# Inverse Fourier slices, token operands and weight parts of a fused Fourier and two-layer expert kernel, placed elsewhere

## The chip, the cores and the metric

The kernel runs on one core of a Trainium2 chip. The metric is the time on the device in microseconds (us) of one execution, compared by the median of several runs. The core has TensorE (PE in the profile, with its weight loads as PEld), VectorE (DVE), ScalarE (ACT), GpSimd (POOL) and SyncE (SP), which issues all the DMAs of this kernel. Each engine executes its instructions in order.

## The reference

The input `x` is 2 sequences of 3008 rows of 256 numbers. Three things are computed one after the other:

```python
X = np.fft.rfft(x, axis=1)                       # 1. Fourier, complex 256x256 product, shrink, inverse
Yr = Xr @ w_r - Xi @ w_i + b_r ; Yi = Xr @ w_i + Xi @ w_r + b_i
Y = sign(Y) * max(abs(Y) - 0.01, 0)              # real and imaginary part each
x = np.fft.irfft(Y, n=3008, axis=1).reshape(6016, 256)
h = x @ w_in ; x = (h * cos(h)) @ w_out          # 2. first layer, 256 -> 2048 -> 256
h = x @ w_in2 ; out = (h * clip(h + 3, 0, 6) / 6) @ w_out2   # 3. second layer
```

The weights of both layers arrive as 64-bit floats and are converted on the chip.

## The kernel before

**Precision.** A large matrix product is made of three fp32r products: each operand is split in a high part (ACT copies it, which rounds) and a low part (the operand less the high part, one subtraction), and high x high, high x low and low x high are added (`three`, line 754).

**Stage one** (up to about 178 us) holds the forward transform and most of the inverse one. It runs 24 rounds `k2_step(i)`, each with `w_mm` (tile `pp`), `b_mm` (`bp`), `v_mm` (`vp`) and the shrinking between them. What is left of the inverse transform is its last stage: 16 groups `g` of 376 tokens, each in two slices `(g, ec)` of 128 channels. `y_mm` (line 351) makes a slice with four matmuls from `u_sb[g]` and the table `tg_sb[g]` into a PSUM bank, `y_out` (line 363) copies it out on ACT (`yo`), stores it to `x_dram`, and after the second slice of a group issues the loads of `u_sb` and `tg_sb` for the next group (`load_u`). `u_sb` and `tg_sb` have one buffer each. Groups 0 to 4 are done in rounds 16 to 20 of stage one (`Y_EARLY`), the others in stage two.

**Stage two** is the first layer: units `k` = 0 to 47, eight for each of six tiles `jj` of 1024 (the last 896) tokens. A unit has four steps `x` = 0 to 3. In a step `plain(k, x)` makes one block of `h` in PSUM bank `x` with six matmuls; `blk.first()` reads it (ACT L731, DVE L732); the block before it gets its `second()` (ACT Sin L740, DVE product L741, the last reader of its bank); the block two before gets its `split()` (ACT `gh` L747, POOL `gl`); and the block four before is multiplied by the output weights (`out_mm`, tile `acc`, six matmuls). The slices of groups 5 to 15 come one to a unit, in units 1 to 22: `y_mm` in step 2 behind `out_mm`, into bank 0, and `y_out` at the end of step 3. Bank 0 is the bank of the next unit's first block.

**Stage three** (from about 759 us) is the second layer: units 48 to 95, in which seven products replace eight (`seven`): `one()`, `two()` and `last()` fill four banks `h_a` to `h_d`, with sums on DVE between them (L793), and four `out_mm` stand between these.

**Token operands.** `operands(jj)` (line 383) makes the split operands `tok` of the next tile from its staged tokens `st`, in pieces that `prepare(k)` issues in units 3 to 7 of a tile. For a tile of the first layer there are four ACT copies and four subtractions (`halve`); for one of the second layer also sums of tokens: one copy of 512 columns and three of 1024 on ACT, seven `halve` and four subtractions into `st`. All subtractions are `pool_sub` (line 158), so POOL's, and show as L159.

**Weight parts.** `convert` (line 166) turns 512 columns of 64-bit floats into fp32 with DVE bit operations and one POOL sum, and then splits them: `hi()` (ACT L237), `lo()` (POOL), `store()` to DRAM. A part of input weights is split after two such chunks, as 1024 columns in the first layer and 1792 in the second, where four sums of parts come in too (`S1` to `S4`). The `Converter` (line 252) does a chunk in five steps; `cv.step` is called at fixed places in stage one and once in every step of stage two. A chunk's split is done in the third to fifth step of the next chunk. `w_loads(k)` loads the converted weights back, and `require` runs steps until a part is stored. The tile `whi` has one buffer.

**Order.** PE, ACT and SP are in `manual_schedule`: they issue in the order of the program. DVE's and POOL's order is set by the framework's planner from estimated costs.

The lines in question are these:

```python
                if x == 2 and y_late and k > 0:                      # L898
                    y = y_late.pop(0)
                    y_mm(*y, bank(0, f"yp{y[0]}_{y[1]}"))
                elif x == 3 and yp_t:
                    y_out(*y)
```

Of the kernel before, what the change touches and what calls it, by code (L numbers as in the profile page):

```python
# [14 lines left out]
AF = mybir.ActivationFunctionType  # L15
ALU = mybir.AluOpType
# [32 lines left out]
RATE_W = ((2, 1, 2), (0, 0, 1), (0, 1, 1))  # L49
XB, NBIG = 3, 4  # L50
STAGED = [0] * 9 + [1, 2, 4, 5, 7, 8, 10] + [12] * 10
Y_EARLY = range(16, 21)
BIAS_DVE = range(13, 22)


# [67 lines left out]
def fourier_moe_moe_kernel(ctx, tc, x, w_r, w_i, b_r, b_i, ta, tg, fg, win1, wout1, win2, wout2, out):  # L123
# [3 lines left out]
    def f32(ap):  # L127
        return ap.bitcast(F32)
# [29 lines left out]
    def pool_sub(out, x, y):  # L158
        nc.gpsimd.tensor_tensor(out, x, y, op=ALU.subtract)  # L159

    def pool_add(out, x, y):
        nc.gpsimd.tensor_tensor(out, x, y, op=ALU.add)  # L162

    w32 = {}

    def convert(kind, m, c, k):
# [35 lines left out]
        def rest():  # L202
            dve.scalar_tensor_tensor(b, w_lo, float(2.0**-52), b, op0=ALU.mult, op1=ALU.mult)  # L203
            if kind == "o":
                pool_add(a, a, b)
                return
            if k == 0:
                w32[m, c] = persist.tile([128, 8, 256], F32, tag="w32", bufs=1, name=f"w32_{m}{c}")
            w = w32[m, c]
            dst = w[:, A21 : A11 + 1] if k == 0 else w[:, A22 : A12 + 1]  # L210
            pool_add(dst, a.rearrange("p (s f) -> p s f", s=2), b.rearrange("p (s f) -> p s f", s=2))
            if k == 1 and m == 1:
                pool_add(w[:, S1], w[:, A21], w[:, A22])
                pool_sub(w[:, S2], w[:, S1], w[:, A11])
                pool_sub(w[:, S3], w[:, A11], w[:, A21])
                pool_sub(w[:, S4], w[:, A12], w[:, S2])

        def hi():
            if kind == "i":
                s0, ns = SLOTS[m]  # L220
                src = w32[m, c][:, s0 : s0 + ns]
                if direct:
                    t = wi_tile(m, c)
                    dst, low = t[:, 0], t[:, 1]
                else:
                    dst = persist.tile([128, 7, 256], F32R, tag="whi", bufs=1, name=f"whi{name}")[:, :ns]
                    low = src.bitcast(F32R)
            else:
                src = a
                if direct:  # L230
                    t = wo_tile(m, k).rearrange("p z f e -> p z (f e)")
                    dst, low = t[:, 0], t[:, 1]
                else:
                    t = persist.tile([128, 2, 512], F32R, tag="whi", bufs=1, name=f"whi{name}")
                    dst, low = t[:, 0], t[:, 1]
            halves.update(src=src, hi=dst, lo=low)
            act.activation(dst, src, AF.Copy)  # L237

        def lo():
            pool_sub(halves["lo"], halves["src"], f32(halves["hi"]))  # L240

        def store():
            if direct:
# [3 lines left out]
                t = f32(t)  # L247
                sp.dma_start(at[:, z], t.rearrange("p s f -> p (s f)") if kind == "i" else t)

        return dict(load=load, magnitude=magnitude, clamp=clamp, shift=shift, top=top, exponent=exponent, rest=rest, hi=hi, lo=lo, store=store, split=(kind, k) != ("i", 0))  # L250

    class Converter:


        def __init__(self):
            self.queue, self.loaded = [], []
            self.finished = set()
            self.prev, self.last = None, None
            self.course = iter(())

        def add(self, m):
# [9 lines left out]
                ops["load"]()  # L271
                self.loaded.append((key, ops))

        def low(self):
            prev, self.prev = self.prev, None
            if prev:
                prev[1]["lo"]()
                self.last = prev

        def store(self):  # L280
            last, self.last = self.last, None
            if last:
                last[1]["store"]()
                self.finished.add(last[0])

        def chunk(self):
            if self.loaded:
                key, ops = self.loaded.pop(0)
                if not self.prev:
                    ops["magnitude"]()  # L290
                ops["clamp"]()
                yield
                ops["shift"]()
                yield
                ops["top"]()
                if self.prev:
                    self.prev[1]["hi"]()
                yield
                ops["exponent"]()
                self.low()  # L300
                yield
                ops["rest"]()
                self.store()
                if self.loaded:
                    self.loaded[0][1]["magnitude"]()
                yield
                if ops["split"]:
                    self.prev = (key, ops)
                self.load()
            elif self.prev:  # L310
                self.prev[1]["hi"]()
                yield
                self.low()
                yield
                self.store()

        def step(self, n):
            for _ in range(n):
# [64 lines left out]
    def operands(jj):  # L383
# [11 lines left out]
        def at(z, t, count=1):  # L395
            return z[:, t - s0] if count == 1 else z[:, t - s0 : t - s0 + count]

        def halve(t, src):
            pool_sub(at(lo, t), src, f32(at(hi, t)))

        if jj < NJ:
            for e, t in ((0, B11), (1, B21), (0, B12), (1, B22)):
# [8 lines left out]
        halve(B21, st[:, 1, 0])  # L411
        yield
        halve(B22, st[:, 1, 1])
        pool_sub(st[:, 0, 0], st[:, 0, 1], st[:, 0, 0])
        yield
        pool_sub(st[:, 0, 1], st[:, 1, 1], st[:, 0, 1])
        pool_sub(st[:, 1, 1], st[:, 1, 1], st[:, 0, 0])
        act.activation(at(hi, T1, 2), st[:, 0], AF.Copy)
        yield
        pool_sub(st[:, 1, 0], st[:, 1, 0], st[:, 1, 1])  # L420
        halve(T1, st[:, 0, 0])
        halve(T3, st[:, 0, 1])
        act.activation(at(hi, T4, 2), st[:, 1], AF.Copy)  # L423
# [287 lines left out]
    with tc.manual_schedule(engines={mybir.EngineType.PE, mybir.EngineType.SP, mybir.EngineType.Activation}):  # L711
# [39 lines left out]
        def bank(z, name):  # L751
            return psum.tile([128, 512], F32, tag=f"h{z}", bufs=1, name=name)
# [14 lines left out]
        def plain(k, x):  # L767

            f, t = divmod(x, 2)
            h = bank(x, f"h{k}_{x}")  # L770
            blk = Block(k, f, t, h)
            three(h, weights(k, (A11, A21)[f]), tokens(k, (B11, B12)[t]), True, False, blk.n)
            three(h, weights(k, (A12, A22)[f]), tokens(k, (B21, B22)[t]), False, True, blk.n)
            return blk
# [107 lines left out]
        for k in range(G):  # L882
            prepare(k)
            for x in range(4):
                blk = plain(k, x)
                old.append(blk)
                blk.first()
                if len(old) > 2:
                    old[-3].split()
                if len(old) > 1:  # L890
                    old[-2].second()
                for f in pend[:2]:
                    f()
                pend = pend[2:]
                cv.step(1)
                if len(old) > 4:
                    out_mm(old.pop(0))
                if x == 2 and y_late and k > 0:  # L898
                    y = y_late.pop(0)
                    y_mm(*y, bank(0, f"yp{y[0]}_{y[1]}"))  # L900
                elif x == 3 and yp_t:
                    y_out(*y)
            w_loads(k)
        for k in range(G, 2 * G):
            blks, one, two, last = seven(k)
# [71 lines left out]
```

## Time and profile before

| What | Value |
|---|---|
| Median of 3 runs | 1270.52 us (1261.76 to 1274.73) |
| Profiled execution, time on the device | 1268.6 us |
| Its span | 1266.7 us |
| PE busy | 1207.4 us (95%) |
| ACT busy | 774.7 us (61%) |
| POOL busy | 711.7 us (56%) |
| DVE busy | 658.2 us (52%) |
| Chain that ended last | PE 84%, ACT 5%, DMA 4%, POOL 3% |

The span is the time from the first to the last instruction in the trace; the time on the device also holds what lies around it. A busy share is a mean over stages, so the rows below are taken stage by stage. In a timeline row stand the start, the duration, the engine, the line, the operation with the tile written and the tiles read, the shape, the count, and in brackets the idle time before it and what ended that. A row with several instructions of a kind in a row is one merged entry. PE's instructions overlap: a matmul that shows 0.39 us is followed by the next after 0.23.

### The profile page before, as it was taken

The numbers are of one execution on the slowest core, as the hardware profiler recorded it, in microseconds if no ns is written. First come the engines' busy times: TensorE is split into PE (matmuls) and PEld (weight loads), VectorE is DVE, ScalarE is ACT, GpSimd is POOL, SyncE is SP. The second block draws the span as 40 slices with busy tenths as digits, with TensorE's granted clock in tenths as the row PEclk, the third lists the DMA queues.
The fourth block names the chain that finished last, engine by engine and source line by source line (L and its number), as shares of the span: only waits on it lengthen the run. The fifth ranks groups of instructions, "written<-read, shape, count | busy, mean of one in ns | idle before, by whom it ended". The sixth has DMA issues, their size and how long they took to land.

```text
span 1266.7 us, 15833 instructions
## 1 busy us (share of the span) xinstructions
PE 1207.4 (95%) x5520; PEld 1003.9 (79%) x5522; DVE 658.2 (52%) x1007; ACT 774.7 (61%) x1418; POOL 711.7 (56%) x562
## 2 busy tenths in 40 slices
PE   8999899888998989999999899999999999999998
PEld 7888777777776767888888888788787787887897
DVE  3877476755555655555555444444444444444443
ACT  3777476656665666666666565565565665565655
POOL 0434145764666566455454664765756747657644
PEclk9999899999998999999999999999999999999999
DMA  9644666633434412201001442001010010010000
GB/s 243 180 133 125 198 192 226 224 135 110 154 118 134 147 53 101 67 1 37 27 1 65 154 170 107 1 15 52 1 68 0 1 67 1 1 63 1 34 1 29
DMA packets 48007, 108.78 MB, mean 86 GB/s; under 512 B 5972, under 2 KB 22360, under 8 KB 47416
## 3 DMA queue, kind: packets, MB, share of 16 engines
q1 hardware_dynamic: 47928, 107.78, 26.4%
q8 instruction: 43, 0.70, 0.2%
q14 instruction: 36, 0.29, 0.1%
HBM read 65.16 MB, written 42.60 MB: 85 GB/s over the span
## 4 chain that ended last, share of the span: by engine, by line
PE 84%; ACT 5%; DMA 4%; POOL 3%; issue 2%; DVE 1%; SPq 0%; ACTq 0%; POOLq 0%; DVEq 0%
PE acc L756 36%; PE h L756 20%; PE h_b L756 7%; PE pp L541 5%; PE h_a L756 4%; PE h_c L756 2%; PE h_d L756 2%; PE yp L355 2%; PE bp L568 2%; POOL tok L159 2%; PE zp L468 1%; PE vp L607 1%; POOL gl L159 1%; ACT r L740 1%; ACT gh L747 1%
## 5 line engine op out<-in xcount | busy, mean ns | idle before, releaser
L159 POOL TENSOR_TENSOR gl<-r,gh 128x512 fp32r<-128x512 f32 (+1 forms) x384 | 485.2, 1272 | 352.6 <-ACT gh L747 295.1
L756 PE MATMUL acc<-gh,wo 128*128 128x512 f32 (+1 forms) x1536 | 526.9, 389 | 0.0
L756 PEld LDWEIGHTS acc<-gh,wo 128*128 128x128 f32 x1536 | 291.3, 190 | 55.1
L756 PE MATMUL h<-tok,wi 128*128 128x512 f32 (+1 forms) x1152 | 296.7, 393 | 28.5 <-ACT yo L365 28.5
L756 PE MATMUL acc<-gl,wo 128*128 128x512 f32 (+1 forms) x768 | 300.3, 391 | 14.5 <-POOL gl L159 14.5
L756 PEld LDWEIGHTS h<-tok,wi 128*128 128x128 f32 x1152 | 215.6, 190 | 76.8 <-ACT yo L365 37.8
L731 ACT ACTIVATE r<-h 128x512 int32<-128x512 f32 (+1 forms) x192 | 113.0, 589 | 205.5 <-PE h L756 197.0
L732 DVE SCALAR_TENSOR_TENSOR r<-r,h 128x512 f32<-128x512 int32 (+1 forms) x192 | 129.7, 675 | 201.5 <-ACT r L731 201.4
L747 ACT ACTIVATE gh<-r 128x512 fp32r<-128x512 f32 (+1 forms) x384 | 231.2, 615 | 2.7 <-DVE r L741 2.6
L756 PEld LDWEIGHTS acc<-gl,wo 128*128 128x128 f32 x768 | 145.8, 190 | 48.7 <-POOL gl L159 21.5
L741 DVE TENSOR_TENSOR r<-r,h 128x512 f32<-128x512 f32 (+1 forms) x192 | 129.7, 676 | 58.9 <-ACT r L740 58.8
L756 PE MATMUL h_b<-tok,wi 128*128 128x512 f32 (+1 forms) x432 | 120.1, 386 | 0.5 <-DVE h_d L793 0.5
L740 ACT ACTIVATE r<-r 128x512 f32<-128x512 f32 (+1 forms) x192 | 117.8, 613 | 0.0
L159 POOL TENSOR_TENSOR tok<-st,tok 128x512 fp32r<-128x512 f32 (+1 forms) x66 | 83.3, 1274 | 46.6 <-ACT tok L423 14.2
L793 DVE TENSOR_TENSOR h_b<-p,h_b 128x512 f32<-128x512 f32 (+1 forms) x48 | 32.9, 685 | 129.6 <-PE h_b L756 116.8
L756 PEld LDWEIGHTS h_b<-tok,wi 128*128 128x128 f32 x432 | 80.6, 188 | 16.9 <-DVE h_d L793 2.2
L756 PE MATMUL h_a<-tok,wi 128*128 128x512 f32 (+1 forms) x288 | 80.0, 386 | 0.0
L789 ACT ACTIVATE p<-h_a 128x512 f32<-128x512 f32 (+1 forms) x48 | 28.3, 590 | 74.3 <-PE h_a L756 74.3
L756 PEld LDWEIGHTS h_a<-tok,wi 128*128 128x128 f32 x288 | 54.4, 189 | 10.3
L735 DVE SCALAR_TENSOR_TENSOR r<-r,h_a 128x512 f32<-128x512 f32 (+1 forms) x48 | 32.4, 676 | 54.1 <-ACT r L734 54.1
L735 DVE SCALAR_TENSOR_TENSOR r<-r,h_b 128x512 f32<-128x512 f32 (+1 forms) x48 | 32.5, 677 | 54.0 <-ACT r L734 54.0
L162 POOL TENSOR_TENSOR w<-cvai,cvbi 128x512 f32<-128x512 f32 x16 | 21.2, 1324 | 68.0 <-DVE cvbi L203 65.7
(100 smaller groups left out, 1385.1 us busy)
## 6 DMA issues: line engine op xcount, KB each, us to landing
st<-x_dram SPq DMA_DIRECT2D x20, 512.0 KB, 5.5
rawi<-in_win_dram SPq DMA_DIRECT2D x16, 512.0 KB, 4.3
rawo<-in_wout_dram SPq DMA_DIRECT2D x16, 512.0 KB, 4.5
wo_dram<-whio SPq DMA_DIRECT2D x28, 256.0 KB, 2.0
wo<-wo_dram SPq DMA_DIRECT2D x14, 512.0 KB, 6.2
wi<-wi_dram SPq DMA_DIRECT2D x4, 1792.0 KB, 7.0
u_dram<-v SPq DMA_DIRECT2D x48, 128.0 KB, 2.4
u_sb<-u_dram SPq DMA_DIRECT2D x16, 384.0 KB, 4.4
```

What stands on the lines that cost most here:

```text
L159: nc.gpsimd.tensor_tensor(out, x, y, op=ALU.subtract)
L355: pe.matmul(yp[:, i * TP : (i + 1) * TP], lhsT=u_sb[g][:, i, ec * 128 : (ec + 1) * 128], rhs=tg_sb[g][:, i * TP : (i + 1) * TP], start=Tru ...
L541: pe.matmul(pp.rearrange("p a e -> p (a e)"), lhsT=za[:, p, kc, 2 * (k2 % 2) : 2 * (k2 % 2) + 2, :].rearrange("p r n -> p (r n)"), rhs=wb[ ...
L731: act.activation(q, h, AF.Copy, bias=0.25, scale=1.0 / TWO_PI)
L732: dve.scalar_tensor_tensor(r, q, -TWO_PI, h, op0=ALU.mult, op1=ALU.add)
L735: dve.scalar_tensor_tensor(r, r, 6.0, h, op0=ALU.min, op1=ALU.mult)
L740: act.activation(r, r, AF.Sin, bias=math.pi / 2, scale=1.0)
L741: dve.tensor_tensor(r, r, self.h[:, : self.n], op=ALU.mult)
L747: act.activation(gh[:, :n], self.r[:, :n], AF.Copy)
L756: pe.matmul(h[:, :n], lhsT=w, rhs=x, start=start and j == 0, stop=stop and j == 2, skip_group_check=True)
L789: act.activation(r[:, :n], h[:, :n], AF.Copy)
L793: dve.tensor_tensor(h[:, :n], r[:, :n], x[:, :n], op=ALU.add)
```

## The change

1. `Y_EARLY` becomes rounds 16 to 18: groups 0 to 2 stay in stage one, groups 3 to 15 go to stage two.
2. In stage two a unit takes two slices, in steps 1 and 2, from unit 0 on: `y_mm` follows `plain` at once, into bank 3 in step 1 and bank 0 in step 2, and `y_out` follows in the same step, behind `second`. The 26 slices fill units 0 to 12.
3. The subtractions in `operands` go from POOL to DVE.
4. A chunk's split begins in the first step of the next chunk. Input weights are split in pieces of two slots (512 columns), one piece a step, each piece's POOL subtraction issued one step behind its ACT copy. The four sums of a second-layer part take one step each. `store` comes behind the last subtraction. `magnitude` is issued once for every chunk; before, the second chunk of a part had it twice.

```diff
-Y_EARLY = range(16, 21)
+Y_EARLY = range(16, 19)
...
-            if k == 1 and m == 1:
-                pool_add(w[:, S1], w[:, A21], w[:, A22])
-                pool_sub(w[:, S2], w[:, S1], w[:, A11])
-                pool_sub(w[:, S3], w[:, A11], w[:, A21])
-                pool_sub(w[:, S4], w[:, A12], w[:, S2])
+        def sums():
+            if kind == "i" and k == 1 and m == 1:
+                w = w32[m, c]
+                for op, z, x, y in ((pool_add, S1, A21, A22), (pool_sub, S2, S1, A11), (pool_sub, S3, A11, A21), (pool_sub, S4, A12, S2)):
+                    op(w[:, z], w[:, x], w[:, y])
+                    yield
...
-            act.activation(dst, src, AF.Copy)
-        def lo():
-            pool_sub(halves["lo"], halves["src"], f32(halves["hi"]))
+        def pieces():
+            place()
+            src, hi, lo = (halves[z] for z in ("src", "hi", "lo"))
+            last = None
+            for z in range(0, src.shape[1], 2) if kind == "i" else (None,):
+                cut = (lambda t: t[:, z : min(z + 2, src.shape[1])]) if kind == "i" else (lambda t: t)
+                if last:
+                    pool_sub(*last)
+                act.activation(cut(hi), cut(src), AF.Copy)
+                last = cut(lo), cut(src), f32(cut(hi))
+                yield
+            pool_sub(*last)
+            yield
+            store()
...
         def chunk(self):
+            tail = self.tail()
             if self.loaded:
                 key, ops = self.loaded.pop(0)
-                if not self.prev:
+                if not self.begun:
                     ops["magnitude"]()
...
+                for part in ("clamp", "shift", "top", "exponent", "rest"):
+                    ops[part]()
+                    next(tail, None)
+                    if part == "rest":
+                        for _ in tail:
+                            pass
+                        if self.loaded:
+                            self.loaded[0][1]["magnitude"]()
+                    yield
+                self.begun = bool(self.loaded)
+                yield from ops["sums"]()
...
+        def sub(out, x, y):
+            dve.tensor_tensor(out, x, y, op=ALU.subtract)
         def halve(t, src):
-            pool_sub(at(lo, t), src, f32(at(hi, t)))
+            sub(at(lo, t), src, f32(at(hi, t)))
...
                 blk = plain(k, x)
+                y = y_late.pop(0) if y_late and x in (1, 2) else None
+                if y:
+                    y_mm(*y, bank(3 if x == 1 else 0, f"yp{y[0]}_{y[1]}"))
                 old.append(blk)
                 blk.first()
                 if len(old) > 2:
                     old[-3].split()
                 if len(old) > 1:
                     old[-2].second()
+                if y:
+                    y_out(*y)
...
-                if x == 2 and y_late and k > 0:
-                    y = y_late.pop(0)
-                    y_mm(*y, bank(0, f"yp{y[0]}_{y[1]}"))
-                elif x == 3 and yp_t:
-                    y_out(*y)
```

`tail()` runs the `pieces()` of the chunk before and marks it as finished when `store` has been issued. The four other `pool_sub` in `operands` (those into `st`) become `sub` in the same way.

## Rows read from the trace of the kernel before

**Rows 1.** Busy time by stretch: start and end, length, each engine's busy time, granted clock.

```profile
200.00:300.00 100.00, 89.09 (x396) 71.32 (x395) 63.42 (x92) 61.52 (x112) 65.86 (x50) 0.97 0.53 179
500.00:600.00 100.00, 100.00 (x443) 82.81 (x442) 50.54 (x74) 66.43 (x124) 53.74 (x42) 1.00 0.10 35
```

**Rows 2.** What PE waited for in the whole span: total us, times, longest.

```profile
PE h L756 <- ACT yo L365: 28.5, 22, 3.3
PE acc L756 <- POOL gl L159: 14.5, 10, 2.4
PE yp L355 <- DMA tg_sb<-in_tg_dram: 4.5, 3, 2.0
```

**Rows 3.** Timeline of PE, starts of units 2 and 23 and the steps around.

```profile
196.58 1.66 PE L756 MATMUL h<-tok,wi 128*128 128x512 f32 x6 [0.78 <-ACT yo L365]
...
483.86 1.03 PE L355 MATMUL yp<-tg_sb,u_sb 96*128 96x94 f32 x8
...
486.14 0.40 PE L756 MATMUL acc<-gh,wo 128*128 128x512 f32 x1
...
488.46 1.66 PE L756 MATMUL h<-tok,wi 128*128 128x512 f32 x6 [0.78 <-ACT yo L365]
...
491.32 1.52 PE L756 MATMUL h<-tok,wi 128*128 128x512 f32 x6
...
494.04 1.52 PE L756 MATMUL h<-tok,wi 128*128 128x512 f32 x6
```

**Rows 4.** Timeline of all engines in stage two, around steps and slices.

```profile
199.44 1.52 PE L756 MATMUL h<-tok,wi 128*128 128x512 f32 x6
...
202.73 0.69 DVE L741 TENSOR_TENSOR r<-r,h 128x512 f32<-128x512 f32 x1 [0.35 <-ACT r L740]
...
208.95 0.47 ACT L365 ACTIVATE yo<-yp 128x376 f32<-128x376 f32 x1
...
210.78 0.41 SPq L346 DMA_DIRECT2D tg_sb<-in_tg_dram  x1
...
259.20 1.13 PE L355 MATMUL yp<-tg_sb,u_sb 96*128 96x94 f32 x8 [0.57 <-DVE r L741]
```

**Rows 5.** The tile `tg_sb`: its sixteen loads, from issue to landing.

```profile
DMA to landing us min/median/max: 3.8/4.3/4.8
```

**Rows 6.** Timeline of PE in the last rounds of stage one.

```profile
140.41 0.47 PE L541 MATMUL pp<-wh,zh 128*128 128x512 f32 x1
...
147.25 3.41 PE L355 MATMUL yp<-tg_sb,u_sb 96*128 96x94 f32 x16 [1.79 <-DMA tg_sb<-in_tg_dram]
...
158.88 0.48 PE L541 MATMUL pp<-wh,zh 128*128 128x512 f32 x1
...
163.75 0.39 PE L541 MATMUL pp<-wh,zh 128*128 128x512 f32 x1
...
176.20 1.43 PE L568 MATMUL bp<-ph,fgr 128*128 128x512 f32 x5 [0.95 <-DVE ph L555]
```

**Rows 7.** The chain that ended last, stage three: start, duration, work; one row a unit.

```profile
786.05 2.72 PE acc L756 x12
796.25 2.72 PE acc L756 x12
...
1160.82 2.72 PE acc L756 x12
```

**Rows 8.** Timeline at the end of stage two and in stage three, POOL and PE.

```profile
721.96 0.48 PE L756 MATMUL acc<-gl,wo 128*128 128x448 f32 x1 [2.40 <-POOL gl L159]
...
804.93 2.53 POOL L159 TENSOR_TENSOR tok<-st,tok 128x512 fp32r<-128x512 f32 x2
...
808.73 0.50 PE L756 MATMUL acc<-gl,wo 128*128 128x512 f32 x1 [2.05 <-POOL gl L159]
```

**Rows 9.** Line 601, `sl` on DVE: count, shortest, median and longest in ns.

```profile
L601 DVE TENSOR_TENSOR sl<-u,sh x24: 677/692/1940, 41.1 to 180.9; 128x512 fp32r<-128x512 f32 x24
```

**Rows 10.** Groups by shape: the subtraction of second-layer input weights on POOL.

```profile
L159 POOL TENSOR_TENSOR w<-w,whii 128x1792 fp32r<-128x1792 f32 x4 | 16.2, 4038 | 3.6 <-ACT whii L237 3.6
```

More of the change, by code (lines that the diff above doesn't have):

```diff
@@ L211, in rest, with place @@
             pool_add(dst, a.rearrange("p (s f) -> p s f", s=2), b.rearrange("p (s f) -> p s f", s=2))
-            if k == 1 and m == 1:
-                pool_add(w[:, S1], w[:, A21], w[:, A22])
-                pool_sub(w[:, S2], w[:, S1], w[:, A11])
-                pool_sub(w[:, S3], w[:, A11], w[:, A21])
-                pool_sub(w[:, S4], w[:, A12], w[:, S2])
-        def hi():
+        def sums():
[4 more added lines that the diff above has]
+                    yield
+        def place():
             if kind == "i":
@@ L248, in store @@
                 sp.dma_start(at[:, z], t.rearrange("p s f -> p (s f)") if kind == "i" else t)
-        return dict(load=load, magnitude=magnitude, clamp=clamp, shift=shift, top=top, exponent=exponent, rest=rest, hi=hi, lo=lo, store=store, split=(kind, k) != ("i", 0))
+        return dict(load=load, magnitude=magnitude, clamp=clamp, shift=shift, top=top, exponent=exponent, rest=rest, pieces=pieces, sums=sums, split=(kind, k) != ("i", 0))
     class Converter:
@@ L257, in __init__ @@
             self.finished = set()
-            self.prev, self.last = None, None
+            self.prev, self.begun = None, False
             self.course = iter(())
@@ L272, in load, with tail @@
                 self.loaded.append((key, ops))
-        def low(self):
+        def tail(self):
             prev, self.prev = self.prev, None
             if prev:
[L277 to L284, printed above, removed]
+                yield from prev[1]["pieces"]()
+                self.finished.add(prev[0])
         def chunk(self):
+            tail = self.tail()
             if self.loaded:
                 key, ops = self.loaded.pop(0)
-                if not self.prev:
+                if not self.begun:
                     ops["magnitude"]()
[L291 to L306, printed above, removed]
+                for part in ("clamp", "shift", "top", "exponent", "rest"):
[9 more added lines that the diff above has]
+                yield from ops["sums"]()
                 if ops["split"]:
@@ L309, in chunk @@
                 self.load()
[L310 to L315, printed above, removed]
+            else:
+                yield from tail
         def step(self, n):
@@ L413, in operands @@
         halve(B22, st[:, 1, 1])
[L414 removed]
+        sub(st[:, 0, 0], st[:, 0, 1], st[:, 0, 0])
         yield
[L416 to L417 removed]
+        sub(st[:, 0, 1], st[:, 1, 1], st[:, 0, 1])
+        sub(st[:, 1, 1], st[:, 1, 1], st[:, 0, 0])
         act.activation(at(hi, T1, 2), st[:, 0], AF.Copy)
         yield
[L420 removed]
+        sub(st[:, 1, 0], st[:, 1, 0], st[:, 1, 1])
         halve(T1, st[:, 0, 0])
```

## The prediction

> **What bounds the kernel now.** I read the busy shares by stretch first, then what TensorE (PE) waited for, then the timeline of single units. From 500 to 600 us PE is busy all the time; between 200 and 300 us it is busy for 89.09 us of 100, while VectorE, ScalarE and GpSimd (DVE, ACT, POOL) are at 62 to 66 [rows 1]. So PE is the bound throughout, and only its idle time and what follows from it can be won. The list of PE's waits names three that this change touches: 28.5 us in 22 waits for the copy `yo` on ACT, 14.5 us in 10 waits for `gl` on POOL, 4.5 us in 3 waits for the table `tg_sb` [rows 2].
>
> The named wait is not its whole price. In stage two a step without a y slice takes 494.04 - 491.32 = 2.72 us, so a unit of four steps 10.88. A y slice adds 486.14 - 483.86 = 2.28 less the 1.36 us (half a step) of the six `h` matmuls behind it, so 0.92: a unit with one slice should take 11.80. Unit 2 begins at 196.58 and unit 23 at 488.46: 21 units in 291.88 us, 13.90 each [rows 3]. The excess is 2.10 us a unit, of which the named wait is 28.5 / 22 = 1.30. The other 0.80 is the pipeline running empty and filling again, a few waits for DVE and POOL, and slower matmuls after long waits (granted clock 0.97 in the mean [rows 1]).
>
> **The change part by part.** Sums are made against the profiled execution: 1268.6 us, 1.9 above its span of 1266.7 and 1.9 below the median of the three runs.
>
> *y slices.* Before, the copy was the last ACT work of step 3 while the next unit's first block needs the same PSUM bank 0 at once. Now slices sit in steps 1 and 2, their copies are issued in the same step, and the banks (3, then 0) are needed again only two steps later, over 5 us. The 22 waits go, with the excess around them: 22 x 2.10 = **-46.2**. What is late next? First, bank 3 at step 1: its last reader is the DVE product (L741) of the block before, issued one step earlier. In a quiet stretch, counted from a step's first matmul at 199.44, that product ends at 203.42 and `plain` of the next step ends issuing at 199.44 + 2.72 + 1.36 = 203.52: a margin of 0.1 us, and one such wait of 0.57 is already there at 259.20 [rows 4]. Weight conversion or a token operand ahead of L741 on DVE turns it into a wait. Bounds: nothing, or 1.30 for each of 26 slices (the old wait's size), 34. I take 0.4 at the 13 step-1 slices, **+5**, near the one row that shows it; at step 2 the slice just before gives DVE 0.92 more. Second, the loads of the next group: each group now has one unit, and `u_sb` and `tg_sb` have one buffer. The copy will start when the Sin pass ends, about 202.7 on the same scale; from the copy's start to the issue of `tg_sb` SP took 210.78 - 208.95 = 1.83 us behind two stores [rows 4], and landing takes 4.3 us, at most 4.8 [rows 5]. So the table is there at 208.8 to 209.3; PE wants it one slice and six half steps after 200.8, at 209.9. Margin 1.1 to 0.6. Ahead of this load on SP stand the converter's raw loads and stores and, after units 0, 2 and 4, the weight loads, each waiting for its own producer. Bounds 0 and 12 x 2.0 (the longest such wait in rows 2); I take 12 x 0.25 = **+3**.
>
> *Four slices moved from stage one.* They cost 4 x 0.92 = **+3.7** later. In stage one the two rounds that lose them took 158.88 - 140.41 = 18.47 us, one with a wait of 1.79 for the table and then slow matmuls (3.41 for 16); the round after them, without a slice, took 163.75 - 158.88 = 4.87 [rows 6]. That gives back 18.47 - 9.74 = **-8.7**. The two earlier waits for the table stay.
>
> *Token operands.* 90 subtractions (66 into `tok`, 24 into `st`) leave POOL for DVE. In stage three, POOL does the two `tok` ones at 804.93 for 2.53 us, ahead of a `gl` that PE needs, and PE waits 2.05 us at 808.73; there are five such places [rows 8]. From 796.25 to 1160.82 stand 34 units of 796.25 - 786.05 = 10.20 us, 346.8, in 364.57 us: 17.8 lost [rows 7]. With POOL holding nothing but `gl`, `gl` follows its copy. DVE gets 11 subtractions a tile; the nearest row with the same operands, `sl`, has a median of 0.692 and a maximum of 1.940 us [rows 9]. DVE is the engine whose `h_c` sum the last product of a unit waits on, so a group of them placed ahead of that sum is the next delay. DVE's order is the planner's, not the program's, as POOL's was, so the group may be pulled together. Bounds -17.8 and 0; I take 1 us a tile as given back: **-12.8**. The same at the end of stage two: the wait of 2.40 at 721.96 [rows 8] goes, **-2.4**. At the end of stage one four halves join a DVE for which PE already waits 0.95 at 176.20 [rows 6], but the same four leave a POOL that they held: bounds -1 and +5, I take **+2**.
>
> The `sl` row shows the dispute: its median is 0.692, and the 1.940 runs beside a POOL subtraction [rows 9]. The Trainium skill ("SBUF — State Buffer", section "Who interferes with whom") says that a VectorE instruction with two SBUF inputs and a GpSimd instruction that reads SBUF exclude each other, whichever began first holding the pair of ports; by that each moved subtraction can also hold up a `gl`, which no token work on DVE did before, and the token term would shrink towards 0. Median against maximum speaks for a collision in a minority of cases.
>
> *Weight parts.* A POOL piece of 1792 columns, 4.038 us, four times [rows 10], becomes pieces of 512 and one of 256, and the four sums of a second-layer part come one a step; a `gl` no longer queues behind 4 us. PE's `gl` waits in stage two are few, so this gains little. Copies (Abs) issued twice fall away, off the path. Against it: the first piece's ACT copy now comes one step behind the POOL sum that it reads, where it came three steps behind; in rounds 2 to 7 of stage one both are issued in one call, so ACT, in order, waits there with the next `ph` copy behind it. And a second-layer part's `whi` buffer is claimed again one step after its store is issued. PE's four rotating banks cover a microsecond or two of that. Four more converter steps per second-layer part make conversion end about five units later, still eleven before its weights are wanted; the converter's forced steps at unit 4 fall from five to three. Bounds -3 and +6; I take **+2**.
>
> Sum: -46.2 + 5 + 3 + 3.7 - 8.7 - 12.8 - 2.4 + 2 + 2 = -54.4: 1214.2 on 1268.6, so **1216** against the median.
>
> **The rivals.**
> 1. *The bank wait takes the copy's place.* DVE's L741 is late at both slices of a unit. For it: the margin of 0.1 and the 0.57 at 259.20. Against: the wait is bounded by DVE's one product, and step 2 has a margin of about 1 us. At 1.30 x 26 = 34 instead of 5: 1245. Chance 0.12.
> 2. *DVE becomes the late engine.* The token group, at up to 1.940 each, delays the `h_c` sums and the new `gl`; stage three and the end of stage two gain nothing: 1216 + 15.2 = 1231. For it: POOL's order had just such groups. Against: DVE's share there is under half and a subtraction costs half of POOL's. Chance 0.20.
> 3. *Only the named waits go.* The 0.80 a unit beyond the wait belongs to other engines and stays: 22 x 0.80 = 17.6 back, 1234. Chance 0.15.
> 4. *Slower: late group loads.* Twelve loads in line on SP, behind stores that wait for POOL. It passes the old time when each load is late by 54.4 / 12 = 4.5 us beyond my 0.25, and slower by 1% at 5.6; at 6 us it is 1216 + 72 = 1288. For it: one unit per group instead of two. Against: landings of 4.3 us with little spread and a margin of 1. Chance 0.05; a partial form (2 us each, 1240) lies in the range.
>
> My forecast's case has 0.48. The range is **1200 to 1243**: low, no new waits (-8) and -5 more of the third stage's loss; high, rivals 2 and 3 and the milder half of rival 1. Changes under 1% can't be told from none here. Faster by over 1%: 0.89; within 1%: 0.06, where two rivals add up; slower: 0.05.
>
> **What would show it.** After the change, PE's waits hold no `h` behind `yo`; units with two slices take about 12.7 + 0.6 us and there are 13 of them; the units after them take 10.88. A wait of `yp` for `r` L741 in over half of the slices at over 1 us is rival 1; `yp` waiting for `tg_sb` or `u_sb` in most units is rival 4. In stage three no `acc` behind `gl` and tiles about 82 us apart; `h_b` or `acc` waiting behind DVE is rival 2. If stage one does not shorten by about 7 us, the moved subtractions or the earlier copies cost there. The forecast is wrong if the 13.90 us units stay above 12.9 without slices in them.

## The result, and the profile after

The kernel after takes **1215.47 us** (median of 4 runs, 1211.86 to 1221.14), where the runs of the kernel before beside it have a median of 1266.14: ratio 0.96, interval 0.9524 to 0.9677. The profiled execution took 1211.86 us with a span of 1210.1, so its span is 56.6 us shorter; the sum had said 54.4. By the medians 50.7 us are gained, and 55.1 when the kernel after was run a second time (experiment 10).

The page after: the lines to set against the small table of before. DVE has gained 84 us of work and POOL has lost 98, ACT is much as it was, and POOL is gone from the chain. PE does the same 5520 matmuls in 17.8 us less (1207.4 before), with a mean granted clock of 0.997 in place of 0.987; so of the 56.6 us some 39 are idle time of PE and the rest are faster matmuls.

```profile
PE 1189.6 (98%) x5520; PEld 995.8 (82%) x5522; DVE 742.1 (61%) x1097; ACT 770.5 (64%) x1426; POOL 613.4 (51%) x488
PE 85%; DVE 6%; DMA 5%; ACT 2%; issue 1%; SPq 0%; ACTq 0%; DVEq 0%
```

What PE waited for in the whole span after (total us, times, longest). Against [rows 2]: the 28.5 us for `yo` are gone, the 14.5 for `gl` too. The first row is the bank wait that the prediction named (PE waits for the last reader of the bank that a slice needs).

```profile
PE yp L354 <- DVE r L743: 6.0, 5, 2.4
...
PE h_b L758 <- DVE h_d L795: 2.1, 5, 0.5
PE yp L354 <- DMA tg_sb<-in_tg_dram: 1.5, 2, 1.0
PE h_d L805 <- DVE r L743: 1.4, 1, 1.4
```

Busy time by stretch after (columns as in [rows 1]): the stretch that had 10.91 us of idle PE has 5.70. In the third row, six microseconds that begin just before the longest bank wait ends, the granted clock is 0.72.

```profile
200.00:300.00 100.00, 94.30 (x452) 77.88 (x451) 60.35 (x86) 63.07 (x121) 57.98 (x47) 0.97 0.61 201
500.00:600.00 100.00, 100.00 (x443) 82.80 (x442) 54.17 (x79) 65.07 (x121) 49.04 (x39) 1.00 0.08 26
234.00:240.00 6.00, 5.43 (x22) 4.48 (x22) 5.92 (x8) 2.21 (x4) 3.79 (x3) 0.72 0.66 179
```

PE's timeline after. The first and last rows are marks used below: the first output product (in unit 1) and the last stage's first wait in unit 48. Between them stand the slice behind the one with the longest wait (239.91, used further down), a unit with two slices, 329.90 - 317.11 = 12.79 us from slice to slice, and a step without one, 341.35 - 338.63 = 2.72.

```profile
176.31 0.39 PE L758 MATMUL acc<-gh,wo 128*128 128x512 f32 x1
...
239.91 1.02 PE L354 MATMUL yp<-tg_sb,u_sb 96*128 96x94 f32 x8
...
317.11 1.08 PE L354 MATMUL yp<-tg_sb,u_sb 96*128 96x94 f32 x8
...
329.90 1.08 PE L354 MATMUL yp<-tg_sb,u_sb 96*128 96x94 f32 x8
...
338.63 1.52 PE L758 MATMUL h<-tok,wi 128*128 128x512 f32 x6
...
341.35 1.52 PE L758 MATMUL h<-tok,wi 128*128 128x512 f32 x6
...
714.10 0.50 PE L805 MATMUL h_d<-tok,wi 128*128 128x512 f32 x1 [1.42 <-DVE r L743]
```

The chain that ended last, stage three after: the 34 units of [rows 7] now take 1103.79 - 750.99 = 352.8 us, where they took 364.57 and 346.8 would be the floor.

```profile
750.99 2.72 PE acc L758 x12
...
1103.79 2.72 PE acc L758 x12
```

With these marks every run can be cut into three stretches: **stage one** up to the first output product (unit 0, with its two slices after the change, lies in it, which the description of the kernel before counts to stage two), **stage two** from there to the wait in unit 48, **stage three** from there to the end. This table has the profiled execution of each kernel; "idle" is the length of stage two less PE's busy time in it. The kernel after, run a second time, gave 537.84 for stage two against 537.79. That they agree so well is partly luck, since the idle time in it differs by 1.3 and the matmuls by as much the other way; stage one repeats less well (experiment 7 says why). Every row is one execution, on several chips, and the profiled one of the kernel before took 1268.6, where its runs beside the four changes tried on their own have a median of 1264.46. So these four rows gain 4 to 8 us more over the first row, all stages together, than their medians do.

| Kernel | Stage one | Stage two | idle in it | Stage three |
|---|---|---|---|---|
| before | 185.2 | 573.75 | 35.0 | 507.8 |
| slices alone | 181.1 | 555.01 | 18.1 | 505.3 |
| copy alone | 186.2 | 548.79 | 15.8 | 506.2 |
| tokens alone | 182.6 | 564.49 | 30.7 | 496.5 |
| weight parts alone | 183.2 | 571.08 | 35.2 | 507.3 |
| slices + tokens | 178.7 | 557.30 | 21.0 | 495.5 |
| slices + weight parts | 179.6 | 543.50 | 10.8 | 507.0 |
| **after** (all three) | 176.3 | 537.79 | 7.3 | 496.0 |
| after, again | 177.4 | 537.84 | 8.6 | 497.3 |
| after, weights uncut | 187.1 | 540.74 | 10.6 | 497.2 |
| after, `st` on POOL | 179.4 | 538.92 | 8.7 | 500.7 |
| after, slices later | 180.8 | 532.13 | 5.0 | 495.8 |
| after, steps spread | 178.9 | 534.81 | 6.0 | 495.7 |
| **after, later + spread** | 179.1 | 529.21 | 2.7 | 495.9 |

### The profile page after: what moved, and what is told of

It is laid out like the page before. It is cut to its first block, busy times and chain, and to the rows that moved or that the text cites. A ratio compares the mean times of both kernels' runs of the same rounds, so it can differ in the third digit from the quotient of the medians.

```text
span 1210.1 us, 15853 instructions
## 1 busy us (share of the span) xinstructions
PE 1189.6 (98%) x5520; PEld 995.8 (82%) x5522; DVE 742.1 (61%) x1097; ACT 770.5 (64%) x1426; POOL 613.4 (51%) x488
## 4 chain that ended last, share of the span: by engine, by line
PE 85%; DVE 6%; DMA 5%; ACT 2%; issue 1%; SPq 0%; ACTq 0%; DVEq 0%
PE acc L758 38%; PE h L758 20%; PE h_b L758 7%; PE h_a L758 4%; PE pp L543 4%; PE h_d L758 2%; PE h_c L758 2%; PE yp L354 2%; PE bp L570 2%; DVE tok L398 1%; DVE st L398 1%; PE vp L609 1%; DVE r L737 1%; PE zp L470 1%; DMA x_big<-in_ta_dram 1%
## 5 line engine op out<-in xcount | busy, mean ns | idle before, releaser
L159 POOL TENSOR_TENSOR gl<-r,gh 128x512 fp32r<-128x512 f32 (+1 forms) x384 | 492.7, 1291 | 439.3 <-ACT gh L749 387.1
L758 PE MATMUL acc<-gl,wo 128*128 128x512 f32 (+1 forms) x768 | 296.7, 386 | 0.0
L758 PE MATMUL h<-tok,wi 128*128 128x512 f32 (+1 forms) x1152 | 290.0, 387 | 0.0
L398 DVE TENSOR_TENSOR tok<-st,tok 128x512 fp32r<-128x512 f32 (+1 forms) x66 | 62.1, 954 | 4.6 <-ACT tok L406 1.7
```

Source lines behind the costliest of these rows:

```text
L398: dve.tensor_tensor(out, x, y, op=ALU.subtract)
L758: pe.matmul(h[:, :n], lhsT=w, rhs=x, start=start and j == 0, stop=stop and j == 2, skip_group_check=True)
```

## The experiments

Ratios are against runs of the kernel before made beside them on the same chip, with 95% intervals; diffs are against the kernel named. Lists of PE's waits in stage two count from 165 us on (178 with the copy alone), so that they hold unit 0.

**1. Slices alone** (against before: `Y_EARLY` and the loop of stage two).

```
-Y_EARLY = range(16, 21)
+Y_EARLY = range(16, 19)
+                y = y_late.pop(0) if y_late and x in (1, 2) else None
+                if y:
+                    y_mm(*y, bank(3 if x == 1 else 0, ...))
...
+                if y:
+                    y_out(*y)
-                if x == 2 and y_late and k > 0: ...
-                elif x == 3 and yp_t: ...
```

> Of the whole change only the slices: groups 0 to 2 early, two slices a unit in steps 1 and 2. Theory A (the whole excess of 2.10 us a unit comes from the copy that holds bank 0): 42 to 46 us faster, ratio 0.964 to 0.967, no wait of h for yo, units after unit 12 at 10.88 us. Theory B (only the named 1.30 us a unit goes, the other engines own the rest): 24 to 28 us faster, ratio near 0.98. Both: the waits of PE for gl of 10 us in the second layer stay.

Measured: 1244.97 us, 0.9854 (0.983 to 0.9878). Neither number was met; at 1.5% the gain is under half of what the slices' terms had said (-43 us with stage one, 3.4%). PE's waits in stage two, slices alone:

```profile
PE yp L355 <- DVE r L741: 9.1, 6, 4.7
PE acc L756 <- POOL gl L159: 5.6, 4, 2.5
PE yp L355 <- DMA tg_sb<-in_tg_dram: 2.2, 1, 2.2
```

The `yo` wait is gone as foreseen; 16.9 us of other waits stand in its place, where before had 5.1 (4.5 for `gl`, 0.6 for L741) besides the `yo` ones. Around the longest, all engines, slices alone:

```profile
238.47 0.63 ACT L237 ACTIVATE whio<-cvao 128x512 fp32r<-128x512 f32 x1 [2.51 <-DMA wo_dram<-whio]
...
240.35 0.67 ACT L188 ACTIVATE cvai<-rawi 128x512 f32<-128x512 f32 x1 [1.24 <-POOL w L162]
...
242.05 0.69 DVE L732 SCALAR_TENSOR_TENSOR r<-r,h 128x512 f32<-128x512 int32 x1 [3.07 <-ACT r L731]
...
243.82 2.02 PE L355 MATMUL yp<-tg_sb,u_sb 96*128 96x94 f32 x8 [4.71 <-DVE r L741]
```

ACT, in order, stands 2.51 us for a `whio` buffer whose store has not ended and 1.24 for a POOL sum; both are converter work, issued in a burst because unit 4's part is due. The block's own ACT work stands behind them, DVE waits for it, and PE for DVE. The slice then runs at half speed (2.02 against 1.03, granted clock 0.50). That the `yo` waits of the kernel before covered such bursts is inferred, not shown.

**2. The copy alone** (against before: still one slice a unit, in step 2, but made right behind the block's matmuls, ahead of the output product, and copied in the same step).

```
+                y = y_late.pop(0) if y_late and x == 2 and k > 0 else None
+                if y:
+                    y_mm(*y, bank(0, ...))
...
+                if y:
+                    y_out(*y)
-                if x == 2 and y_late and k > 0: ...
-                elif x == 3 and yp_t: ...
```

> One edit to the kernel before: one slice a unit as before (units 1 to 22, step 2, bank 0), but it is made right behind the block's matmuls and copied in the same step; groups 0 to 4 stay early. Theory A (the place of the copy is the cause, not how many slices a unit has): 36 to 44 us faster, ratio 0.966 to 0.972, units 1 to 22 at 11.8 us. Rival (the wait moves to the bank's last reader on DVE): 22 waits of yp for L741 at about 1.3 us, under 10 us faster, ratio above 0.992.

Measured: 1243.2 us, 0.9846 (0.9819 to 0.9873), between the two expectations and as good as two slices a unit. So the gain comes from where the slice is made and copied, not from putting two into a unit. Made and copied earlier are one edit here; in experiment 9 ("later") the matmuls are behind the output product again, only the copy stays earlier, and no `yo` wait returns. Timeline of PE with the copy alone:

```profile
191.89 1.13 PE L355 MATMUL yp<-tg_sb,u_sb 96*128 96x94 f32 x8
...
203.80 1.08 PE L355 MATMUL yp<-tg_sb,u_sb 96*128 96x94 f32 x8
...
244.82 2.02 PE L355 MATMUL yp<-tg_sb,u_sb 96*128 96x94 f32 x8 [5.25 <-DVE r L741]
```

A quiet unit takes 203.80 - 191.89 = 11.91, near the 11.80 of the prediction, so there the whole excess did go. But stage two is only 25.0 us shorter, not 46.2, and its waits say why (copy alone):

```profile
PE yp L355 <- DVE r L741: 9.2, 4, 5.3
PE acc L756 <- POOL gl L159: 4.9, 4, 2.4
```

**3. Tokens alone** (against before; likewise in the four lines that write `st`).

```
+        def sub(out, x, y):
+            dve.tensor_tensor(out, x, y, op=ALU.subtract)
         def halve(t, src):
-            pool_sub(at(lo, t), src, f32(at(hi, t)))
+            sub(at(lo, t), src, f32(at(hi, t)))
```

> Only the token subtractions go from POOL to DVE. Theory A: about 14 us faster (11.8 in the second layer as in the changed kernel, 2.4 at the end of the first), ratio 0.989, and the waits of h for yo stay at about 28 us in 22 places. Rival (two subtractions on DVE and POOL exclude each other and DVE becomes late): within 3 us of before, ratio 0.998 to 1.002, gl late as before.

Measured: 1249.04 us, 0.9885 (0.9858 to 0.9911), as expected. PE's waits with tokens alone, whole span: the `gl` waits of 14.5 us are down to 0.3, `yo` stays, and the price on DVE is the last row. Three token subtractions on DVE take 3.78 to 3.83 us, each beside a POOL weight subtraction of 4.01 to 4.06; no bank wait of PE comes of it here, other than in experiment 5.

```profile
PE h L759 <- ACT yo L365: 28.9, 22, 3.3
...
PE h_b L759 <- DVE h_d L796: 2.4, 6, 0.5
```

**4. Weight parts alone** (against before: `place`, `pieces`, `sums` and the converter's `chunk` and `tail` as in the change's diff, nothing else of it).

```
-                if self.prev:
-                    self.prev[1]["hi"]()
...
+                for part in ("clamp", "shift", "top", "exponent", "rest"):
+                    ops[part]()
+                    next(tail, None)
...
+                yield from ops["sums"]()
```

> Only the weight parts in pieces, one step earlier. Theory A (nearly nothing, the few long yo waits behind the 1.7 us ACT copy get shorter): 0 to 6 us faster, ratio 0.995 to 1.0. Rival (the ACT copy right behind the POOL sum stalls stage one): slower by 3 to 8 us, ratio 1.002 to 1.006. Third theory (the stall of POOL by 4 us parts was a large part of the excess in stage two): over 10 us faster, ratio below 0.992.

Measured: 1263.28 us, 0.9994 (0.9975 to 1.0012): nothing, as expected. Its `yo` waits are the old ones, 30.4 us in 22:

```profile
PE h L755 <- ACT yo L364: 30.4, 22, 5.1
PE acc L755 <- POOL gl L159: 13.4, 9, 2.4
```

The three singles together give 1.46 + 1.15 + 0.06 = 2.67%, the whole 4.0%. So some parts do something together that none does alone; the pairs say which.

**5. Slices + tokens** (against after: the weight parts' functions back as before).

```
-                    next(tail, None)
-                yield from ops["sums"]()
...
+                if self.prev:
+                    self.prev[1]["hi"]()
...
+                self.low()
```

> Slices and token operands changed, weight parts as before. The slices alone were 1.5% faster, the tokens 1.2%, the weight parts 0.1%, the whole 4.0%: some 1.3% exist only together. Theory A (the earlier, smaller weight pieces shorten the waits of the slices for L741): this kernel gets 30 to 36 us of the whole 51, ratio 0.972 to 0.976, with a wait of yp near 4.7 us at unit 5 as in the slices alone. Theory B (it is POOL's relief that the slices need): 45 us or more, ratio below 0.966, no wait over 2.5 us there.

Measured: 1232.97 us, 0.9718 (0.9697 to 0.974), as theory A said. By time the two about add up (2.6% from the singles, 2.8% here), but not by stage: in stage two this kernel is 2.3 us longer than slices alone, though tokens alone had taken 9.3 off there. PE's waits in stage two, slices + tokens, and the timeline of one:

```profile
PE yp L355 <- DVE r L744: 16.6, 5, 4.9
PE acc L759 <- POOL gl L159: 2.4, 3, 1.5
```

```profile
266.30 4.01 POOL L159 TENSOR_TENSOR w<-w,whii 128x1792 fp32r<-128x1792 f32 x1 [0.77 <-ACT whii L237]
...
266.77 4.09 DVE L399 TENSOR_TENSOR tok<-st,tok 128x512 fp32r<-128x512 f32 x1 [1.42 <-ACT tok L407]
...
272.11 1.41 PE L355 MATMUL yp<-tg_sb,u_sb 96*128 96x94 f32 x8 [3.77 <-DVE r L744]
```

POOL's uncut weight subtraction runs from 266.30 to 270.31, and the token subtraction on DVE, 0.69 at its median, ends at 270.86, after 4.09 us. The next L744 is late and PE stands 3.77. The same three rows return at 340.47, 340.88 and 346.28 (4.01, 4.15 and 3.84 us). These two waits are most of what the tokens add, where slices alone has 0.70 at each; of the others, 4.92 at unit 5 and 2.78 at unit 9 were there with slices alone (4.71 and 2.54). This is the exclusion that the prediction cited from the Trainium skill ("SBUF — State Buffer", section "Who interferes with whom"); the trace agrees, and shows it at its most expensive: the DVE instruction ends 0.55 us after the POOL one, whenever it began.

**6. Slices + weight parts** (against after: the token operands back on POOL, those of `st` too).

```
-            sub(at(lo, t), src, f32(at(hi, t)))
+            pool_sub(at(lo, t), src, f32(at(hi, t)))
```

> Slices and weight parts changed, token subtractions on POOL as before. Theory A: the whole less what the tokens give alone, 34 to 38 us faster, ratio 0.970 to 0.973, with gl late in the second layer as before and no gl wait in the slices' units. Theory B: about 20 us faster, ratio 0.983 to 0.986.

Measured: 1232.03 us, 0.9714 (0.9691 to 0.9738), as theory A said, where 1 and 4 would add to 1.5%: weight parts alone show 2.7 us of stage two, which their time can't tell from nothing, behind moved slices 11.5 (555.01 to 543.50), and with the tokens moved too 19.5 (557.30 to 537.79). Of the 11.5, 7.3 are idle time of PE and 4.2 faster matmuls. PE's waits in stage two, slices + weight parts:

```profile
PE yp L354 <- DVE r L740: 5.0, 4, 2.8
PE acc L755 <- POOL gl L159: 3.4, 2, 2.4
PE yp L354 <- DMA tg_sb<-in_tg_dram: 1.1, 1, 1.1
```

**7. After, weights uncut** (against after: the steps in their new places, each POOL and ACT instruction in one piece).

```
-            for z in range(0, src.shape[1], 2) if kind == "i" else (None,):
-                cut = (lambda t: t[:, z : min(z + 2, src.shape[1])]) if ...
+            for z in (None,):
+                cut = lambda t: t
```

> The changed kernel with the input weights of a part split in one ACT copy and one POOL subtraction of 1024 or 1792 columns, all else of the new order kept. Theory (a subtraction with two SBUF operands on DVE waits out the POOL instruction beside it, 4.0 us at 1792 columns, so the pieces are what the token operands on DVE need): 7 to 14 us slower than the changed kernel, token subtractions of about 4 us on DVE, waits of yp for L743 over 3 us in two of units 6 to 12. Rival (the gain of the weight part is its earlier place, not the cut): within 2 us of the changed kernel.

Measured: 1224.34 us, 0.9645 (0.9605 to 0.9686), against 1214.11 for the kernel after beside it. Ten microseconds, within the 7 to 14 that were expected, but not for the reason given, and not all of them are the cut's. The profile's first stretch, weights uncut:

```profile
0.00:30.00 30.00, 26.73 (x126) 23.58 (x128) 7.24 (x14) 7.71 (x15) 0.20 (x4) 0.68 0.92 239
```

Its granted clock there is 0.68, where the kernel after had 1.00 and, run again, 0.94, with the same instructions so far. PE's 161st matmul starts at 38.7 us here and at 28.7 in the second run, and its 891st 9.6 us later: the 9.7 us by which stage one is longer than the second run's 177.4 were lost before the first of these. Stage two, where the cut acts, is 2.9 us longer, with four `gl` waits of 2.4 us in all that after does not have; stage three is equal. Two token subtractions took 4.13 and 4.14 us, but stood after the slices, so the long `yp` waits that were expected did not come. The profile shows about 3 us for the cut; the two of its six runs with the highest mean clock (0.996 and 0.995) took 1219.74 and 1220.22, 3 to 7 above the kernel after's 1213.09 to 1216.35. Its full price stays open. What is left of the weight parts' 19.5 us is put down to the steps' new places: sums one a step, pieces from the first step of the next part on, three forced steps at unit 4 instead of five. No run took these apart, so this is argued, but number 9 bears on the forced ones.

**8. After, `st` on POOL** (against after; the four subtractions into `st` alone).

```
-        sub(st[:, 0, 0], st[:, 0, 1], st[:, 0, 0])
+        pool_sub(st[:, 0, 0], st[:, 0, 1], st[:, 0, 0])
...
-        sub(st[:, 1, 0], st[:, 1, 0], st[:, 1, 1])
+        pool_sub(st[:, 1, 0], st[:, 1, 0], st[:, 1, 1])
```

> The changed kernel with the four subtractions into st of each second-layer tile back on POOL, the seven into tok kept on DVE. Theory (in the second layer DVE's group of subtractions now is the late one, 0.48 us at h_b a tile): h_b waits go and up to 3 us are gained. Rival (POOL's order again puts them ahead of gl): waits of acc for gl of about 1 to 2 us in five places, 3 to 9 us slower than the changed kernel.

Measured: 1220.46 us, 0.962 (0.9587 to 0.9652), 6.3 above the kernel after. The size is the rival's, but the wait is another: hardly `gl` (1.5 us in 2), but DVE. Of the 6.4 us between the two profiles 3.4 lie in stage three; 1.9 lie in stage one, which the edit does not touch. PE's largest wait, `st` on POOL, and the timeline of one:

```profile
PE h_b L758 <- DVE h_c L795: 6.2, 4, 1.5
```

```profile
762.04 2.99 POOL L159 TENSOR_TENSOR st<-st 128x512 f32<-128x512 f32 x2 [3.04 <-DVE tok L398]
762.14 3.44 DVE L398 TENSOR_TENSOR tok<-st,tok 128x512 fp32r<-128x512 f32 x2 [0.17 <-ACT tok L411]
...
766.24 0.96 PE L758 MATMUL h_b<-tok,wi 128*128 128x512 f32 x3 [1.54 <-DVE h_c L795]
```

Two DVE subtractions beside two on POOL take 3.44 us, and `h_c`, next on DVE, is late. Splitting the token work over both engines is worse here than giving it all to DVE, though still better than all on POOL (0.962 against the 0.9714 of experiment 6).

**9. After, slices later / steps spread / both** (against after). "Later" puts a slice's matmuls behind the step's output product and its copy at the head of the next step; "spread" runs two converter steps in step 3 of units 1 to 3, so that the three forced at unit 4 run earlier.

```
-                y = y_late.pop(0) if y_late and x in (1, 2) else None
-                if y: y_mm(...)
+                if yp_t:
+                    y_out(*y)
...
-                cv.step(1)
+                cv.step(2 if x == 3 and k in (1, 2, 3) else 1)
                 if len(old) > 4:
                     out_mm(old.pop(0))
+                if y_late and x in (1, 2):
+                    y = y_late.pop(0)
+                    y_mm(...)
```

> The changed kernel, but a slice is made behind the output products of its step and copied at the head of the next step. Theory (the slices wait only for L741 of the block before, a margin of 0.1 us): the five waits of 6.0 us go, 6 to 9 us faster than the changed kernel, 1206 to 1210 us, units of two slices at 12.8 us. Rival (L741 is late because DVE as a whole is late there, and the wait moves to the next user of the bank or to gl): within 2 us of the changed kernel.

> The changed kernel with three more converter steps, in step 3 of units 1, 2 and 3, so that none is forced in one go at unit 4. Theory (the longest wait, 2.40 us at unit 5, and the slower matmuls behind it come from the forced steps): 2 to 4 us faster than the changed kernel. Rival (the steps cost the same wherever they stand): within 1 us, with the wait at another unit.

> Both edits to the changed kernel that were tried singly: slices behind the output products with the copy at the head of the next step, and three converter steps moved into units 1 to 3. Theory (the two remove different waits of the slices): 3 to 6 us faster than the changed kernel. Rival (what is left of the waits is late loads, and the edits do not add): within 2 us of the better single one.

Measured: later 1213.26 (0.9573, 0.9536 to 0.9609), spread 1210.51 (0.9547, 0.9522 to 0.9573). Neither can be told from after (0.9573 in experiment 10) by its time, so the 6 to 9 us and the 2 to 4 us of the theories are not shown; stage two says 5.7 and 3.0 us shorter. Bank waits are down from 6.0 us in 5 to 1.4 in 2 in the later one, and the 2.40 wait at unit 5 is gone in the spread one. The later one's profile lost 4.3 us against after's by PE's 161st matmul (31.6 against 27.3 us), where the two run the same. **Both: 1205.51 us (1202.9 to 1206.9), 0.95 (0.9468 to 0.9532)**, 8.6 below the kernel after beside it (next paragraph), with intervals that don't overlap; more than the 3 to 6 expected, and the fastest version. What is left of PE's waits in stage two, both:

```profile
PE yp L354 <- DVE r L734: 0.6, 1, 0.6
PE yp L354 <- DVE cvai L194: 0.4, 1, 0.4
PE yp L354 <- DVE r L743: 0.3, 1, 0.3
PE yp L354 <- DMA tg_sb<-in_tg_dram: 0.3, 1, 0.3
```

**10. After, again** (the kernel after, unchanged: no diff).

> The changed kernel again, unaltered, so that the three kernels below are compared with it on one chip: 0.955 to 0.965 of the kernel before.

Measured: 1214.11 us (1213.09 to 1216.35), 0.9573 (0.9541 to 0.9605), as expected. Bank waits of 4.8 us in 4, `tg_sb` waits of 2.7 in 3.

## Why the prediction was right, step by step

The total was right and so were stage three and the place of the new wait; the split of stage two was not, and that its sum came out is in part luck: the slices gave 18 us less than forecast, and the weight parts 13 to 21 more. Predicted by the same marks: stage one -4.2 (the moved slices' -8.7, the halves' +2, unit 0's two slices and their waits +2.5), measured -8.9; stage two -37.4 (the weight parts' +2 counted in it), measured -36.0; stage three -12.8, measured -11.8.

- **The step that failed: "the 22 waits go, with the excess around them: 22 x 2.10 = -46.2".** Alone, the moved slices took 18.7 off stage two where the prediction's terms for them there make -37, and the copy alone 25.0, even less than the named 28.5 (by the medians both rather less). The 2.10 was an average over 21 units that differ. Timeline of PE before, the slices of two neighbouring quiet units:

```profile
191.98 1.03 PE L355 MATMUL yp<-tg_sb,u_sb 96*128 96x94 f32 x8
...
204.88 1.03 PE L355 MATMUL yp<-tg_sb,u_sb 96*128 96x94 f32 x8
```

These are 12.90 apart, and 11 of the 21 distances from slice to slice lie between 12.84 and 12.93; the other ten run from 13.45 to 18.11. With the copy alone 14 of 21 lie between 11.85 and 12.05. So the late copy itself cost about 1.0 us a unit, 22 us in 22 units, and what the average held beyond that was lost in units that had other trouble too. The 46.2 was about all that stage two lost to anything: the table has 35.0 us of idle PE before, and the matmuls took 538.8 us where the best version needs 526.5 with two slices more. This is rival 3's mechanism, true of the slices by themselves. The rest needn't even stay the same: with the `yo` waits gone, PE ran into the converter bursts of experiment 1 (16.9 us of other waits in place of 5.1).

- **Weight parts, +2: wrong in sign, and this paid for the first error.** Cut, issued earlier and spread, they took 11.5 to 19.5 off stage two once the slices were moved; which of the three did how much is open. The reason given for the small term ("PE's `gl` waits in stage two are few") held for the kernel before, and the experiment that measures the part alone confirms it (0.9994); it did not ask what PE would wait for once the slices had moved. The cost that I named, ACT waiting in order for a buffer, is there (5.3 us in three waits for `whio` on ACT after), but no row of PE's waits is left that it could stand behind, save the bank waits.
- **Tokens, -12.8 and -2.4: right.** Stage three is 11.8 shorter, no `gl` wait is left, and the price on DVE is small: 2.1 us in 5 waits of `h_b`, 6.0 us over the floor in 34 units against the 5 that I took. In stage two the term is not a constant: -9.3 alone, +2.3 behind the slices, -5.7 behind slices and weight parts (543.50 to 537.79). The +2.3 is the exclusion of experiment 5, a form of rival 2 (DVE late), at the bank and not at `h_c`. In the kernel after it is still seen, but short: 17 of the 66 `tok` subtractions take over 1 us, the longest 1.79.
- **Bank wait, +5: right in place, and in size as far as the named waits go.** 6.0 us in 5 waits (4.8 in 4 in the second run), all but one of 0.3 in stage two. I spread it over 13 slices at 0.4; it came as a few long ones, and behind the two longest the matmuls are slow: the next slice starts 239.91 - 234.56 = 5.35 and 295.22 - 289.89 = 5.33 later, where 333.62 - 329.90 = 3.72 is usual, 3.2 us more in all. So the term was nearer 9 than 5, and 8.6 is what "both" took off. The longest is in unit 5, behind the three converter steps forced at the end of unit 4. There two DVE steps that take 0.43 and 0.69 at their medians took 1.57 and 1.69 beside POOL work. After, all engines:

```profile
229.68 1.29 POOL L159 TENSOR_TENSOR whio<-cvao,whio 128x512 fp32r<-128x512 f32 x1 [0.31 <-ACT whio L248]
229.68 1.57 DVE L194 TENSOR_SCALAR cvai<-cvai 128x512 uint32<-128x512 uint32 x1
...
231.15 1.28 POOL L159 TENSOR_TENSOR gl<-r,gh 128x512 fp32r<-128x512 f32 x1 [0.18 <-ACT gh L749]
231.29 1.69 DVE L197 SCALAR_TENSOR_TENSOR cvai<-rawi,cvai 128x512 uint32<-128x512 uint32 x1
...
234.56 1.13 PE L354 MATMUL yp<-tg_sb,u_sb 96*128 96x94 f32 x8 [2.40 <-DVE r L743]
```

- **Late loads, +3, and rival 4:** 0 us in stage two in the first run (both `tg_sb` waits are in stage one), 2.7 in the second. The margin about held, though the slowest `tg_sb` load landed after 6.8 us (7.3 in the second run), where I had 4.8 at most.
- **Stage one, -8.7 and +2:** 4.7 better than the sum of -4.2. PE's wait for `ph` at the end went from 0.95 to 0.47 instead of growing, and the table waits before it from 4.5 us in 3 to 1.5 in 2; about a microsecond of it goes with the clock of the first 30 us, 0.94 before and 1.00 after; after's second run, with 0.94, is at 177.4, so 7.8 below before.
- **Rival 1** did not come: no wait at most slices, and a unit with two slices takes 12.79, the 12.7 of the forecast.

## What to carry to other kernels

An average excess per unit is what all causes lost together: give it to the wait you remove only in units that show no other wait, and price the rest as what will stand behind it. A part that measures nothing alone may be worth 1% once another part has taken away the wait that covered it, so test parts in pairs, and compare them by stretch: two profiles of one kernel agreed here to a tenth of a microsecond in the stage that mattered, while its runs spread over nine. Their idle times in it still differ by 1.3, so make nothing of a microsecond. When work goes to DVE, look at how long POOL's instructions are; and leave a step between a bank's last reader and its next use.

## What the runs showed of the hardware that was not expected

- With slices and tokens three DVE subtractions of 128x512 took 4.09, 4.15 and 4.19 us beside POOL ones of 4.01 to 4.06, six times their 0.69; the DVE product L744, next but one behind, took 0.67 to 0.68 as always.
- After PE's wait of 4.92 us in the kernel with slices and tokens the granted clock was 0.50, the lower level of 1.2 GHz, for the 3.1 us that follow, so a long wait is paid for again after it ends: the next slice starts 6.33 us after the one that waited, where 3.7 is usual. Busy time by stretch there:

```profile
239.90:243.00 3.10, 3.04 (x11) 2.85 (x12) 3.10 (x6) 1.67 (x4) 1.26 (x1) 0.50 0.41 159
```

- The first 30 us, the same instructions each time, ran at a granted clock of 0.68, 0.94 and 1.00 in three profiled executions (weights uncut, after again, after), and the end of stage one stood at 187.1, 177.4 and 176.3 us: a spread as large as a part of this change is worth.
